# Low parts to VectorE, the residual sum earlier and fused, LayerNorm moments on ScalarE, in a two-block fp32 kernel

## The chip, the cores and the metric

One core of one Trainium2 chip. The metric is the device time of one execution in microseconds (us), the median of three runs. TensorE is PE in the profile, with PEld its weight loads; VectorE is DVE, ScalarE is ACT, GpSimd is POOL, and SyncE, which issues most DMAs, is SP.

## The reference, cut to what matters

Two residual blocks over x of shape (2048, 512), fp32: attention with a learned feature map, then an MLP over the token axis.

```python
h0 = layernorm(x)                                   # over 512 channels, eps 1e-5
q, k, v = split(h0 @ wqkv)                          # 32 heads of 16
phi(u) = concat(softmax(u @ w_phi), softmax(-u @ w_phi))
kv = phi(k)^T v ;  z = sum over tokens of phi(k)
o  = phi(q) kv / (phi(q) . z + 1e-6)
h  = x + o @ wo
u  = gelu(layernorm(h)^T @ w1 + b1)                 # (512, 1792), contraction over 2048 tokens
out = h + (u @ w2 + b2)^T
```

## The kernel before, in words

The 2048 tokens are 16 tiles of 128. Every fp32 product is made of three fp32r matmuls: an operand is split into a high part (a copy by ScalarE, rounded to fp32r) and a low part (operand minus high part), and `mm3` multiplies high by high, high by low and low by high. So every weight and activation costs one copy on ScalarE and one subtraction on VectorE or GpSimd.

The stages, in order: the weights of q, k and v are prepared; a loop over tiles makes the features of k and v and accumulates kv and z; a short stretch ends that loop; the attention loop makes h; then the token MLP runs to the end (w1 to 300 us and beyond, then w2, line 745).

**The end of the k loop.** z is kept as `zacc` (128 x 1024), summed over tiles. The last addition (line 481, VectorE) is followed by two TensorE products with ones (line 486) that sum over partitions, and ScalarE copies the result to `zB` (line 487). Ahead of it in GpSimd's queue stand the low parts of wo for two of its four slices (`wo_lo`, line 429), the other two stand a little later.

**The attention loop** runs `it` from 0 to 18. From the k loop's last call on and through this loop, the order on TensorE, VectorE, ScalarE and GpSimd is the order in which the code calls (a manual schedule); each engine works its queue in order and waits by semaphores. One iteration does a step for several tiles:

- `s_num(it-1)`, line 544: TensorE multiplies transposed features by kv into the PSUM tile `tn`; ScalarE copies the high part `oh` (548); VectorE makes the low part `ol` (553, called in `s_ol`).
- `s_wo(it-2)`: 12 matmuls (lines 61 to 63) of oh, ol with woh, wol into PSUM tile `po`, of which there is one.
- `s_tr(it)`, line 526: TensorE transposes features into `tn`, again one buffer, shared with s_num; so it waits for `ol`. ScalarE copies the result to `pht` (528).
- `lead`: `s_pq` (458, GpSimd multiplies the features by the weights `w`), `s_ez` (440, GpSimd multiplies features by zB), one `negate` (159, GpSimd), the next q projection on TensorE, one exponential on ScalarE (169).
- a list of VectorE steps, interleaved from two lists: `ol`; the reduction `tz` of ez (449) and five small steps that end in `w` (450 to 455); for a projected q tile the maximum `mx` (151), the minimum `mn` (152) and the shift `eq` = q - mx (144); two sums `smq` (214). The shift's other half is a ScalarE copy of the same PSUM tile (`eq`, line 146); it waits for the VectorE half, since both write one tile. Projections of q end when all 16 are made; the last one, of tile 15, is shifted in iteration 5.
- `s_hn(it-3)`: ScalarE normalizes h of tile it-3 into `hn` (583) and copies the high part `hs` (56); GpSimd makes the low part (57). It needs `s_rstd(it-3)`, two GpSimd operations on 128x1 (578, 579) called at the iteration's start.
- `s_h(it-2)`: VectorE adds po to x (line 568, `h`), SP stores it, VectorE takes the moments (571 to 575).
- `fill`: the first w1 products, 6 matmuls for one pair of column blocks and one token tile. Pair 0 starts in iteration 4; pair 1 starts in iteration 5, after the q projections, and takes over the two PSUM tiles `pu` of q tiles 14 and 15.
- `fill_load`: SP loads a piece of w1 (`wraw`), ScalarE makes `whi`, VectorE `wlo` (56, 57), two pieces at the end of iteration 2, one at the end of 4 and of 5, two of 6, and so on.

Of the kernel before, what the change touches and what calls it, by code (L numbers as in the profile page):

```python
# [9 lines left out]
F32 = mybir.dt.float32  # L10
F32R = mybir.dt.float32r
AF = mybir.ActivationFunctionType
ALU = mybir.AluOpType
# [4 lines left out]
P = 128  # L18
S, D, H, DH, F = 2048, 512, 32, 16, 1792
NT = S // P  # L20
KD = D // P
# [8 lines left out]
EPS = 1e-5  # L30
# [3 lines left out]
def block_kernel(ctx: ExitStack, tc: tile.TileContext, x, xT, wT, phic, wo, w1, b1, w2, b2,  # L34
                 kvmask, ident_in, out):
    nc = tc.nc

    cst = ctx.enter_context(tc.tile_pool(name="cst", bufs=1))
# [6 lines left out]
    b1s = cst.tile([P, NF], F32, name="b1s")  # L45
    b2s = cst.tile([P, NT], F32, name="b2s")
    r1 = cst.tile([P, NT], F32, name="r1")
    mv2 = cst.tile([P, NT, 2], F32, name="mv2")
    r2 = cst.tile([P, NT], F32, name="r2")
    cst.tile([P, 56], F32, name="pad")  # L50
    nc.vector.memset(ones, 1.0)
    nc.vector.memset(mhalf, -0.5)

    def split(hi, lo, src, lo_engine):

        nc.scalar.activation(hi, src, AF.Copy)  # L56
        return lo_engine.tensor_sub(lo, src, hi)  # L57

    def mm3(o, ah, al, bh, bl, first, last):

# [27 lines left out]
    zacc = wp.tile([P, NG, P], F32, name="zacc")  # L88
# [5 lines left out]
    X, XH, EQ, PK, VS, SQ, PS, W = {}, {}, {}, {}, {}, {}, {}, {}  # L94
# [41 lines left out]
    def logit_ops(src, e, pool):  # L136

        v = src.rearrange("p (j h d) -> p j h d", h=2, d=DH)
        ev = signs(e)
        mx = wk.tile([P, NPR, 2], F32, name="mx")  # L140
        mn = wk.tile([P, NPR, 2], F32, name="mn")

        def shift():
            nc.vector.tensor_sub(ev[:, :, 0], v, mx.unsqueeze(3).to_broadcast([P, NPR, 2, DH]))
            if pool:
                nc.scalar.activation(ev[:, :, 1], v, AF.Copy)  # L146
                MN.append((ev, mn))
            else:
                nc.vector.tensor_sub(ev[:, :, 1], mn.unsqueeze(3).to_broadcast([P, NPR, 2, DH]), v)

        return [lambda: nc.vector.tensor_reduce(mx, v, axis=AX.X, op=ALU.max),
                lambda: nc.vector.tensor_reduce(mn, v, axis=AX.X, op=ALU.min),
                shift]

    def negate():

        if MN:
            ev, mn = MN.pop(0)
            nc.gpsimd.tensor_sub(ev[:, :, 1], mn.unsqueeze(3).to_broadcast([P, NPR, 2, DH]), ev[:, :, 1])

    def run(*lists):

        for i in range(max(map(len, lists))):
            for ops in lists:
                if i < len(ops):
                    ops[i]()

    def exps(t, e):
        nc.scalar.activation(e, e, AF.Exp, scale=r1[:, t:t + 1])
# [1 line left out]
    def heads(e):  # L171
        return e.rearrange("p g (a d) -> p (g a) d", d=DH)
# [224 lines left out]
    for t in range(3, NT - 1):  # L397
        if t + 2 < NT:
            raw = load_x(t + 2)
# [22 lines left out]
    woh = w2p.tile([P, KD, D], F32R, name="woh")  # L422
    wol = w2p.tile([P, KD, D], F32R, name="wol")
# [2 lines left out]
        nc.scalar.activation(woh[:, j], WO[j], AF.Copy)  # L426

    def wo_lo(j):
        nc.gpsimd.tensor_sub(wol[:, j], WO[j], woh[:, j])

    WO = {}
    for j in range(KD):
# [24 lines left out]
    def s_pq(t):  # L457
        nc.gpsimd.tensor_mul(heads(EQ[t]), heads(EQ[t]), W[t].rearrange("p g c h -> p (g c h)").unsqueeze(2).to_broadcast([P, 2 * H, DH]))  # L458

    def lead(it, mm):  # L460

        if 0 <= it + 1 < NT:
            s_pq(it + 1)
        if 0 <= it + 3 < NT:
            s_ez(it + 3)
        negate()
        for _ in range(mm):
            q_mm()
        q_exp(0)
# [4 lines left out]
    k_norm(NT - 1, False)  # L474
    for j in range(KD):
        wo_hi(j)
    wo_lo(0)
    wo_lo(1)
    v_kv()
    run(q_logits(0))  # L480
    nc.vector.tensor_add(zacc, zacc, PK[NT - 1])
    negate()
    zB = big.tile([P, NG, P], F32, name="zB", tag="big")
    for g in range(2):
# [3 lines left out]
    q_exp(0)  # L488
    s_ez(0)
    s_ez(1)  # L490
    wo_lo(2)
    wo_lo(3)
    q_mm()
    v_kv()
    run(s_den(0))
# [34 lines left out]
    def s_kv():  # L530

        pt = ps_o.tile([P, 2, P], F32, name="po")
        for b in range(2):
            nc.tensor.transpose(pt[:, b, :], kvS[:, 2 * b:2 * b + 2, :].rearrange("p n f -> p (n f)"), ident)
        nc.scalar.activation(kvB, pt, AF.Copy)

    def s_num(t):

        pn = ps_t.tile([P, 2, 4, P], F32, name="tn")[:, :, 0:2]
        for b in range(2):  # L540
            for c in range(4):
                for r in range(2):
                    rows, cols = slice(64 * r, 64 * r + 64), slice(32 * c, 32 * c + 32)
                    nc.tensor.matmul(pn[cols, r, b, :], kvB[rows, b, cols], PHT[t][rows, 4 * b + c, :],  # L544
                                     start=True, stop=True, skip_group_check=True)
        oh = ak.tile([P, 2, 2, P], F32R, name="oh")
        ol = ak.tile([P, 2, 2, P], F32R, name="ol")
        nc.scalar.activation(oh, pn, AF.Copy)
        OS[t] = oh, ol, pn

    def s_ol(t):
        oh, ol, pn = OS[t]
        return [lambda: nc.vector.tensor_sub(ol, pn, oh)]
# [11 lines left out]
    def s_h(t):  # L565

        h = HT[t]
        nc.vector.tensor_add(h, PO.pop(t), h)  # L568
        nc.sync.dma_start(out[t * P:(t + 1) * P, :], h)
        st = ak.tile([P, 6], F32, name="st2")  # L570
        nc.vector.bn_stats(st, h)
        nc.vector.bn_aggr(mv2[:, t, :], st)
        VE[t] = ak.tile([P, 2], F32, name="ve2")
        nc.vector.tensor_scalar(VE[t][:, 0:1], mv2[:, t, 1:2], 1.0 + EPS, EPS * EPS, op0=ALU.mult, op1=ALU.add)
        nc.vector.tensor_scalar_mul(VE[t][:, 1:2], mv2[:, t, 0:1], -1.0)

    def s_rstd(t):
        nc.gpsimd.tensor_tensor(r2[:, t:t + 1], VE[t][:, 0:1], mhalf[:, :1], op=ALU.pow)
        nc.gpsimd.tensor_mul(VE[t][:, 1:2], VE[t][:, 1:2], r2[:, t:t + 1])
# [7 lines left out]
    w1v = w1.rearrange("(k p) f -> p k f", p=P)  # L587
    w2v = w2.rearrange("(k p) s -> p k s", p=P)

    def stream(src, k0, n, c0, w):  # L590

        raw = wf.tile([P, n, w], F32, name="wraw")
        wh_ = wf.tile([P, n, w], F32R, name="whi")
        wl_ = wf.tile([P, n, w], F32R, name="wlo")
        nc.sync.dma_start(raw, src[:, k0:k0 + n, c0:c0 + w])
        LO.append(split(wh_, wl_, raw, nc.vector).ins)
        return wh_, wl_

    PU, WI, LO = {}, {}, []
    FN, FL = [0] * (NF // 2), [0] * (NF // 2)  # L600

    def fill_load(p):
        if FL[p] < NT:
            WI[p, FL[p]] = stream(w1v, FL[p], 2, p * 256, 256)
            FL[p] += 2

    def fill(p, pool=None):

        t = FN[p]
        FN[p] = t + 1  # L610
        if FL[p] <= t:
            fill_load(p)
        if t == 0:
            PU[p] = [pool.tile([P, D], F32, name="pu", tag="pu") for _ in range(2)]
        a, b = WI[p, t - t % 2]
        for c in range(2):
            mm3(PU[p][c], a[:, t % 2, c * P:(c + 1) * P], b[:, t % 2, c * P:(c + 1) * P],
                HN[t][:, 0], HN[t][:, 1], t == 0, t == NT - 1)

    for it in range(NT + 3):  # L620
        if 0 <= it < NT:
            s_x(it)
        if 0 <= it - 3 < NT:
            s_rstd(it - 3)
        if 0 <= it - 1 < NT:
            s_num(it - 1)
        if 0 <= it - 2 < NT:
            s_wo(it - 2)
        if it == 1:
            run(q_logits(0))  # L630
            q_mm()
        if 0 <= it < NT:
            s_tr(it)
        if it == 0:
            s_kv()
        lead(it, 1)
        den = s_den(it + 2) if it + 2 < NT else []
        run((s_ol(it - 1) if 0 <= it - 1 < NT else []) + q_logits(1) + (q_sums(0) if it > 0 else []), den)
        if it > 0:
            negate()  # L640
        if 0 <= it - 3 < NT:
            s_hn(it - 3)
        if 0 <= it - 2 < NT:
            s_h(it - 2)
        if FN[0] <= it - LAG:
            fill(0, ps_f)
        for _ in range(2):
            if q["logits"] == NT and FN[1] <= it - LAG:
                fill(1, ps_q)
        for p in range(2):  # L650
            if it >= LAG - 2 and FL[p] <= FN[p] + 1:
                fill_load(p)
    ms.close()
    a2.close()
    aq.close()
# [100 lines left out]
    for n, (sp, p) in enumerate(STEPS):  # L756
        t = 2 * sp
# [15 lines left out]
        if not last:  # L773
# [6 lines left out]
            for i, add in enumerate((u3.unsqueeze(1).to_broadcast([P, 2, HD]), e)):  # L780
                nc.vector.scalar_tensor_tensor(ot[:, i], bank[2 + i], b2s[:, t + i:t + i + 1], add,  # L781
                                               op0=ALU.add, op1=ALU.add)
# [68 lines left out]
```

## Time and profile before

| | |
|---|---|
| three runs | 535.80, 535.86, 536.12 us; median 535.86 |
| the profiled execution | 535.76 us, of which 534.0 is the span from the first to the last instruction |
| granted TensorE clock, mean | 0.997 of full speed |
| busy: PE, DVE, ACT, POOL | 522.6, 393.5, 258.6, 236.6 us |
| HBM read, written | 46.81, 8.39 MB |

All times in rows are microseconds from the start of the span. A row of the timeline has start, duration, engine, line, operation, the tiles written and read, their shapes, how many instructions in succession it stands for, and in brackets the engine's idle time before it with what ended that. A row of the waits view has the waiting engine and line, what it waited for, the total, the number of waits and the longest.

### The profile page before, as it was taken

The page shows a single profiled execution, that of the slowest core. Times are in us where ns is not written, and L with a number is a line of the kernel's source. Part 1 is how long each engine was busy: PE and PEld are TensorE (multiplying, and loading weights), DVE is VectorE, ACT ScalarE, POOL GpSimd, SP SyncE. Part 2 cuts the span into 40 slices and gives each one's busy share as a digit, 9 for nine tenths or more (in the row PEclk, how much of TensorE's full clock was granted, in tenths as well). Part 3 has the DMA queues.
Part 4 walks back from the last instruction along what each step waited for, and adds up shares of the span by engine and source line. Part 5 has one row for each costly group of instructions (what it writes and reads, how often), then busy time and mean ns, then how long its engine had stood idle before and what let it go on. Part 6 is the DMA issues. An engine that isn't in the chain of part 4 may idle for free.

```text
span 534.0 us, 9892 instructions
## 1 busy us (share of the span) xinstructions
PE 522.6 (98%) x3872; PEld 450.4 (84%) x3872; DVE 393.5 (74%) x722; ACT 258.6 (48%) x406; POOL 236.6 (44%) x184
## 2 busy tenths in 40 slices
PE   8999999998999999999999999999999999999995
PEld 7888888886876777778788888888899999999995
DVE  6993999875699989986536523835768878888774
ACT  6998844434346555544546423525443343343340
POOL 2589699878978989985435000000001101100110
PEclk9999999999999999999999999999999999999998
DMA  8534300021302233333256333533014556536631
GB/s 315 196 113 118 99 21 21 1 78 63 97 4 86 73 101 118 100 121 118 91 166 179 98 100 97 160 107 91 20 41 108 139 149 144 133 119 140 138 80 40
DMA packets 45486, 55.84 MB, mean 105 GB/s; under 512 B 3968, under 2 KB 33024, under 8 KB 45440
## 3 DMA queue, kind: packets, MB, share of 16 engines
q1 hardware_dynamic: 43136, 51.38, 30.2%
q0 software_dynamic: 2016, 3.67, 5.1%
q8 instruction: 30, 0.49, 0.4%
q10 hardware_dynamic: 288, 0.17, 0.1%
q14 instruction: 16, 0.13, 0.1%
HBM read 46.81 MB, written 8.39 MB: 103 GB/s over the span
## 4 chain that ended last, share of the span: by engine, by line
PE 91%; DVE 5%; ACT 2%; issue 1%; POOL 0%; DVEq 0%; POOLq 0%
PE py L745 26%; PE pu L61 12%; PE pu L62 12%; PE pu L63 12%; PE po L61 3%; PE pv L62 3%; PE pv L63 3%; PE pv L61 3%; PE pk_ps L61 2%; PE pk_ps L63 2%; PE pk_ps L62 2%; PE tn L526 2%; PE po L62 2%; PE po L63 2%; PE kvp L205 2%; PE tn L544 1%
## 5 line engine op out<-in xcount | busy, mean ns | idle before, releaser
L57 DVE TENSOR_TENSOR wlo<-wraw,whi 128x512 fp32r<-128x512 f32 (+1 forms) x84 | 100.3, 1204 | 69.4 <-ACT whi L56 67.9
L56 ACT ACTIVATE whi<-wraw 128x512 fp32r<-128x512 f32 (+1 forms) x84 | 81.9, 987 | 127.1 <-PE py L745 73.8
L783 POOL DMA_DIRECT2D out<-ot x14 | 12.5, 1001 | 211.3 <-DVE ot L781 211.3
L745 PE MATMUL py<-uf,whi 128*128 128x256 f32 x560 | 96.2, 283 | 0.0
L61 PE MATMUL pu<-hs,whi 128*128 128x512 f32 x224 | 87.6, 394 | 0.6 <-ACT eq L146 0.6
L62 PE MATMUL pu<-hs,whi 128*128 128x512 f32 x224 | 87.2, 389 | 0.0
L63 PE MATMUL pu<-hs,wlo 128*128 128x512 f32 x224 | 86.8, 389 | 0.0
L745 PEld LDWEIGHTS py<-uf,whi 128*128 128x128 f32 x560 | 83.3, 192 | 0.0
L745 PE MATMUL py<-uf,wlo 128*128 128x256 f32 x280 | 69.9, 283 | 0.0
L61 PEld LDWEIGHTS pu<-hs,whi 128*128 128x128 f32 x224 | 42.1, 188 | 9.5 <-ACT eq L146 1.1
L745 PEld LDWEIGHTS py<-uf,wlo 128*128 128x128 f32 x280 | 49.7, 192 | 0.0
L63 PEld LDWEIGHTS pu<-hs,wlo 128*128 128x128 f32 x224 | 42.0, 188 | 8.8
L62 PEld LDWEIGHTS pu<-hs,whi 128*128 128x128 f32 x224 | 42.1, 188 | 8.2
L528 ACT ACTIVATE pht<-tn 128x512 f32<-128x512 f32 x32 | 17.4, 596 | 49.7 <-PE tn L526 49.7
L440 POOL TENSOR_TENSOR ez<-eq,zB 128x1024 f32<-128x1024 f32 x16 | 38.4, 2406 | 0.7 <-ACT zB L487 0.7
L745 PE MATMUL py<-un,whi 128*128 128x256 f32 x224 | 38.4, 283 | 0.0
L193 POOL TENSOR_TENSOR pk<-pk,sk 128x1024 f32<-128x1024 f32 x16 | 31.1, 1944 | 9.4 <-DVE sk L192 7.6
L745 PEld LDWEIGHTS py<-un,whi 128*128 128x128 f32 x224 | 33.2, 192 | 0.1
L458 POOL TENSOR_TENSOR eq<-eq,w 128x1024 f32<-128x1024 f32 x16 | 31.1, 1942 | 3.1 <-DVE w L455 3.1
L197 POOL TENSOR_TENSOR zacc<-zacc,pk 128x1024 f32<-128x1024 f32 x13 | 31.3, 2409 | 0.6
L57 POOL TENSOR_TENSOR hs<-hn,hs 128x512 fp32r<-128x512 f32 x16 | 20.6, 1291 | 21.1 <-ACT hs L56 21.1
L61 PE MATMUL po<-woh,oh 128*128 128x512 f32 x64 | 26.6, 416 | 1.0 <-DVE h L568 1.0
(161 smaller groups left out, 1144.3 us busy)
## 6 DMA issues: line engine op xcount, KB each, us to landing
wraw<-in_w SPq DMA_DIRECT2D x112, 256.0 KB, 2.8
xraw<-in_xT SPq DMA_DIRECT2D x16, 256.0 KB, 3.1
xh<-in_x SPq DMA_DIRECT2D x16, 256.0 KB, 2.7
h<-in_x SPq DMA_DIRECT2D x16, 256.0 KB, 2.9
out<-h SPq DMA_DIRECT2D x16, 256.0 KB, 2.2
out<-ot POOLq DMA_DIRECT2D x14, 256.0 KB, 4.8
wraw<-in_wT SPq DMA_DIRECT2D x12, 256.0 KB, 4.9
wo<-in_wo SPq DMA_DIRECT2D x4, 256.0 KB, 3.8
```

What stands on the lines that cost most here:

```text
L56: nc.scalar.activation(hi, src, AF.Copy)
L57: return lo_engine.tensor_sub(lo, src, hi)
L61: nc.tensor.matmul(o, ah, bh, start=first, stop=False)
L62: nc.tensor.matmul(o, ah, bl, start=False, stop=False)
L63: nc.tensor.matmul(o, al, bh, start=False, stop=last)
L193: nc.gpsimd.tensor_mul(heads(PK[t]), heads(PK[t]), sk.unsqueeze(2).to_broadcast([P, 2 * H, DH]))
L197: nc.gpsimd.tensor_add(zacc, zacc, PK[t])
L440: nc.gpsimd.tensor_mul(EZ[t], EQ[t], zB)
L458: nc.gpsimd.tensor_mul(heads(EQ[t]), heads(EQ[t]), W[t].rearrange("p g c h -> p (g c h)").unsqueeze(2).to_broadcast([P, 2 * H, DH]))
L528: nc.scalar.activation(PHT[t][:, half * 4:half * 4 + 4, :], ptr[:, half], AF.Copy)
L745: nc.tensor.matmul(o, a[x], b[:, y], start=start and i == 0, stop=stop and i == 2, skip_group_check=True)
L783: nc.gpsimd.dma_start(out[(t + i) * P:(t + i + 1) * P, :], flat(ot[:, i]), accum_op=ALU.add)
```

## The change

Five edits, all at the end of the k loop and in the attention loop.

1. The four low parts of wo are made by VectorE, not GpSimd, after the last addition to zacc; that addition is cut into two halves of 512 columns, one for each of the two products that follow.
2. h is made by one `scalar_tensor_tensor` that also writes the sum of its row (`accum_out`). It stands fourth in VectorE's list, behind ol and two more steps, where it stood behind the whole list.
3. `bn_stats`, `bn_aggr` and two small operations on VectorE go. ScalarE makes the moments in the next iteration (`s_moments`, called between s_num and s_wo, so between oh and pht in ScalarE's queue): one 128x1 copy, one pass of squares over 128x512 with its sum, one 128x1 operation. s_rstd is called behind s_pq.
4. The low parts of w1's pieces are not made when the piece is loaded but a step later (`flush`), directly behind h in VectorE's list, so in the iteration after the load.
5. Bookkeeping: a constant tile, a pad, `s_pq` called outside `lead`.

TensorE's order stays the same up to a few w1 products behind the loop, where the scheduler places them.

```diff
-    def wo_lo(j):
-        nc.gpsimd.tensor_sub(wol[:, j], WO[j], woh[:, j])
+    def wo_lo(j):
+        nc.vector.tensor_sub(wol[:, j], WO[j], woh[:, j])
...
-    wo_lo(0)
-    wo_lo(1)
     v_kv()
     run(q_logits(0))
-    nc.vector.tensor_add(zacc, zacc, PK[NT - 1])
+    for g in range(2):
+        nc.vector.tensor_add(zacc[:, 4 * g:4 * g + 4, :], zacc[:, 4 * g:4 * g + 4, :], PK[NT - 1][:, 4 * g:4 * g + 4, :])
+    for j in range(KD):
+        wo_lo(j)
     negate()
...
     s_ez(1)
-    wo_lo(2)
-    wo_lo(3)
...
     def s_h(t):
         h = HT[t]
-        nc.vector.tensor_add(h, PO.pop(t), h)
+        VE[t] = ak.tile([P, 4], F32, name="ve2", bufs=3)
+        nc.vector.scalar_tensor_tensor(h, PO.pop(t), 1.0, h, op0=ALU.mult, op1=ALU.add, accum_out=VE[t][:, 2:3])
         nc.sync.dma_start(out[t * P:(t + 1) * P, :], h)
-        st = ak.tile([P, 6], F32, name="st2")
-        nc.vector.bn_stats(st, h)
-        nc.vector.bn_aggr(mv2[:, t, :], st)
-        VE[t] = ak.tile([P, 2], F32, name="ve2")
-        nc.vector.tensor_scalar(VE[t][:, 0:1], mv2[:, t, 1:2], 1.0 + EPS, EPS * EPS, op0=ALU.mult, op1=ALU.add)
-        nc.vector.tensor_scalar_mul(VE[t][:, 1:2], mv2[:, t, 0:1], -1.0)
+
+    def s_moments(t):
+        junk = ak.tile([P, D], F32, name="hj", bufs=1)
+        nc.scalar.activation(VE[t][:, 1:2], VE[t][:, 2:3], AF.Copy, scale=-1.0 / D)
+        nc.scalar.activation(junk, HT[t], AF.Square, bias=VE[t][:, 1:2], accum_out=VE[t][:, 3:4])
+        nc.scalar.activation(VE[t][:, 0:1], VE[t][:, 3:4], AF.Identity, scale=(1.0 + EPS) / D, bias=eps2)
...
+    LATER = []
+    def flush():
+        while LATER:
+            wl_, raw, wh_ = LATER.pop(0)
+            LO.append(nc.vector.tensor_sub(wl_, raw, wh_).ins)
...
         nc.sync.dma_start(raw, src[:, k0:k0 + n, c0:c0 + w])
-        LO.append(split(wh_, wl_, raw, nc.vector).ins)
+        nc.scalar.activation(wh_, raw, AF.Copy)
+        LATER.append((wl_, raw, wh_))
...
-        if 0 <= it - 3 < NT:
-            s_rstd(it - 3)
         if 0 <= it - 1 < NT:
             s_num(it - 1)
+        if 0 <= it - 3 < NT:
+            s_moments(it - 3)
         if 0 <= it - 2 < NT:
             s_wo(it - 2)
...
+        if 0 <= it + 1 < NT:
+            s_pq(it + 1)
+        if 0 <= it - 3 < NT:
+            s_rstd(it - 3)
         lead(it, 1)
         den = s_den(it + 2) if it + 2 < NT else []
-        run((s_ol(it - 1) if 0 <= it - 1 < NT else []) + q_logits(1) + (q_sums(0) if it > 0 else []), den)
+        ops = turns((s_ol(it - 1) if 0 <= it - 1 < NT else []) + q_logits(1) + (q_sums(0) if it > 0 else []), den)
+        ops[3:3] = ([lambda: s_h(it - 2)] if 0 <= it - 2 < NT else []) + [flush]
+        run(ops)
         if it > 0:
             negate()
         if 0 <= it - 3 < NT:
             s_hn(it - 3)
-        if 0 <= it - 2 < NT:
-            s_h(it - 2)
```

More of the change, by code (lines that the diff above doesn't have):

```diff
@@ L47, in block_kernel @@
     r1 = cst.tile([P, NT], F32, name="r1")
-    mv2 = cst.tile([P, NT, 2], F32, name="mv2")
+    eps2 = cst.tile([P, 1], F32, name="eps2")
     r2 = cst.tile([P, NT], F32, name="r2")
-    cst.tile([P, 56], F32, name="pad")
+    cst.tile([P, 80], F32, name="pad")
     nc.vector.memset(ones, 1.0)
     nc.vector.memset(mhalf, -0.5)
+    nc.vector.memset(eps2, EPS * EPS)
     def split(hi, lo, src, lo_engine):
         nc.scalar.activation(hi, src, AF.Copy)
-        return lo_engine.tensor_sub(lo, src, hi)
+        lo_engine.tensor_sub(lo, src, hi)
     def mm3(o, ah, al, bh, bl, first, last):
@@ L159, in negate, with turns @@
             nc.gpsimd.tensor_sub(ev[:, :, 1], mn.unsqueeze(3).to_broadcast([P, NPR, 2, DH]), ev[:, :, 1])
+    def turns(*lists):
+        return [ops[i] for i in range(max(map(len, lists))) for ops in lists if i < len(ops)]
     def run(*lists):
[L163 to L166, printed above, removed]
+        for op in turns(*lists):
+            op()
     def exps(t, e):
@@ L460, in lead @@
     def lead(it, mm):
-        if 0 <= it + 1 < NT:
-            s_pq(it + 1)
         if 0 <= it + 3 < NT:
@@ L612, in fill @@
             fill_load(p)
+            flush()
         if t == 0:
@@ L652, in block_kernel @@
                 fill_load(p)
+    flush()
     ms.close()
```

## The prediction

> **What bounds the kernel now.** First the page's line of busy times, then the view of TensorE's waits cut to 115 to 290 us, the stretch that the change touches.
>
> ```profile
> PE 522.6 (98%) x3872; PEld 450.4 (84%) x3872; DVE 393.5 (74%) x722; ACT 258.6 (48%) x406; POOL 236.6 (44%) x184
> PE pk_ps L486 <- DVE zacc L481: 1.7, 1, 1.7
> PE po L61 <- DVE h L568: 1.0, 1, 1.0
> PE pu L61 <- ACT eq L146: 0.6, 1, 0.6
> PE tn L526 <- DVE ol L553: 0.5, 1, 0.5
> ```
>
> TensorE is busy for 522.6 of 534.0 us, and its order and work hardly change. So the gain can only come out of these four waits, 3.8 us together, and a loss only out of waits that the change makes. VectorE's 393.5 us matter only where a step of it is the last that TensorE waits for. I take the four in order of time. "Iteration" means `it`; a is the price, so far unknown, of writing the row sum beside h.
>
> **The end of the k loop.** The timeline there:
>
> ```profile
> 123.96 3.48 POOL L429 TENSOR_TENSOR wol<-wo,woh 128x512 fp32r<-128x512 f32 x2
> 124.03 2.28 DVE L481 TENSOR_TENSOR zacc<-zacc,pk 128x1024 f32<-128x1024 f32 x1
> 126.46 1.96 PE L486 MATMUL pk_ps<-zacc,ones 128*128 128x512 f32 x4 [1.69 <-DVE zacc L481]
> 131.57 1.22 DVE L449 TENSOR_REDUCE tz<-ez 128x64 f32<-128x1024 f32 x1 [5.25 <-POOL ez L440]
> 179.70 1.29 POOL L57 TENSOR_TENSOR hs<-hn,hs 128x512 fp32r<-128x512 f32 x1 [0.30 <-ACT hs L56]
> 180.18 1.36 DVE L57 TENSOR_TENSOR wlo<-wraw,whi 128x512 fp32r<-128x512 f32 x1
> ```
>
> The addition reads two SBUF tiles and takes 2.28 us. The last two rows show another such instruction: wlo starts while GpSimd's hs (179.70 to 180.99) runs and ends at 181.54, 0.55 us after that one's end. So a VectorE subtraction with two SBUF operands makes no headway while GpSimd works on SBUF. The addition at 124.03 overlaps GpSimd's wol in the same way. The change takes wol off GpSimd and cuts the addition in two. A half has 512 columns, for which a subtraction or addition takes 0.68 us (ol, below). TensorE waits for the first half alone: 124.03 + 0.68 + the 0.15 that lay between the addition's end (126.31) and the matmul (126.46) = 124.86, **1.6 us** earlier. The second half is there 0.6 later, before the second product. The four wol subtractions, four times 0.6, go into VectorE's idle time of 5.25 us ahead of tz at 131.57, and GpSimd loses the work. I cost them at nothing; without that cover they would put 2.4 us ahead of tz, which TensorE reaches only through w and the features, iterations later.
>
> From here I give times on the clock of before, without these 1.6 us, and add them in at the end.
>
> **The order within an iteration.** VectorE and ScalarE from 164 us on, iteration 3; the row of 409.09 is the form that h takes, without the sum; then groups of the same operations.
>
> ```profile
> 164.24 1.28 DVE L57 TENSOR_TENSOR wlo<-wraw,whi 128x512 fp32r<-128x512 f32 x2
> 165.44 0.68 DVE L553 TENSOR_TENSOR ol<-tn,oh 128x512 fp32r<-128x512 f32 x1
> 166.04 1.21 DVE L449 TENSOR_REDUCE tz<-ez 128x64 f32<-128x1024 f32 x1
> 167.16 0.68 DVE L151 TENSOR_REDUCE mx<-pu 128x32 f32<-128x512 f32 x1
> 167.76 0.18 DVE L450 SCALAR_TENSOR_TENSOR tz<-smq,tz 128x32 f32<-128x32 f32 x1
> 167.86 0.68 DVE L152 TENSOR_REDUCE mn<-pu 128x32 f32<-128x512 f32 x1
> 168.45 0.22 DVE L452 TENSOR_TENSOR tz<-smq,tz 128x64 f32<-128x64 f32 x1
> 168.59 0.68 DVE L144 TENSOR_TENSOR eq<-pu,mx 128x512 f32<-128x512 f32 x1
> 409.09 0.75 DVE L781 SCALAR_TENSOR_TENSOR ot<-py,b2s,e 128x512 f32<-128x512 f32 x1
> 163.54 0.61 ACT L548 ACTIVATE oh<-tn 128x512 fp32r<-128x512 f32 x1
> 167.43 1.09 ACT L528 ACTIVATE pht<-tn 128x512 f32<-128x512 f32 x2 [3.28 <-PE tn L526]
> 168.40 1.16 ACT L169 ACTIVATE eq<-eq,r 128x1024 f32<-128x1024 f32 x1
> 169.44 0.60 ACT L146 ACTIVATE eq<-pu 128x512 f32<-128x512 f32 x1
> 169.92 0.82 ACT L583 ACTIVATE hn<-h,ve,r 128x512 f32<-128x512 f32 x1
> 170.77 0.63 ACT L56 ACTIVATE hs<-hn 128x512 fp32r<-128x512 f32 x1
> 171.31 0.58 ACT L548 ACTIVATE oh<-tn 128x512 fp32r<-128x512 f32 x1
> L571 DVE BATCH_NORM_STATS2 st<-h 128x6 f32<-128x512 f32 x16 | 11.1, 695 | 0.5
> L113 ACT ACTIVATE sqj<-xh,st 128x512 f32<-128x512 f32 x16 | 11.5, 721 | 0.3
> L113 ACT ACTIVATION_READ_ACCUMULATOR sqj<-xh,st 128x1 f32 x16 | 3.0, 191 | 0.0
> ```
>
> Starts lie 0.6 apart for a 0.68 us instruction, so I add starts, not durations (h: 0.67).
>
> What goes: the moments on VectorE, 0.7 for bn_stats and some 0.4 for three small ones, about 1.1 us in each iteration, at the end of its list. It comes back on ScalarE as 0.72 for the squares, 0.19 for their sum and two operations on 128x1, at most 0.2 each by that last row: 1.3 us between oh and pht, where ScalarE idles 3.28 us now. As oh and pht come closer together below, some 1.9 us remain; cover to spare is 0.5 us, so I cost it at nothing. Without cover the exponential and the copy `eq` (146) would be that much later.
>
> What moves: h goes from behind the list to behind ol, tz and mx; wlo goes from before ol to behind h. So ol is earlier by wlo's time, and shift `eq` (144), and with it ScalarE's copy (146), later by h's 0.67 + a and wlo's 0.6 a piece. That copy is queued ahead of hn, hs, whi and the next oh, and oh is what the next ol and TensorE's next transpose wait for. SP's queue gets h's store earlier, which holds nothing up.
>
> For a, nothing in this profile shows a VectorE instruction that sums beside its output. The nearest rows: no surcharge (0.75 at 409.09), or ScalarE's 0.19 read; the far end is a second pass, 0.6. Nothing suggests less than none. I take 0.05 to 0.1. By itself: the Trainium skill ("VectorE: DVE Perf Modes", section "Two Vector instructions with no wait between them") states that such an operation is two instructions, the main one and a read of the accumulator; no row of before shows one on VectorE, and by it a would be nearer the 0.19.
>
> **Iterations 3 and 4.** GpSimd there, TensorE at two places, and a later pair of wlo:
>
> ```profile
> 162.70 1.06 POOL L159 TENSOR_TENSOR eq<-mn,eq 128x512 f32<-128x512 f32 x1 [1.07 <-ACT eq L146]
> 164.34 0.99 POOL L578 TENSOR_TENSOR r<-ve,mhalf 128x1 f32<-128x1 f32 x1 [0.58 <-DVE ve L575]
> 165.55 1.93 POOL L458 TENSOR_TENSOR eq<-eq,w 128x1024 f32<-128x1024 f32 x1
> 167.45 2.41 POOL L440 TENSOR_TENSOR ez<-eq,zB 128x1024 f32<-128x1024 f32 x1
> 170.12 1.06 POOL L159 TENSOR_TENSOR eq<-mn,eq 128x512 f32<-128x512 f32 x1 [0.26 <-PE pu L63]
> 172.87 0.55 POOL L578 TENSOR_TENSOR r<-ve,mhalf 128x1 f32<-128x1 f32 x1
> 174.57 1.04 PE L526 MATMUL tn<-ident,eq 128*128 128x128 f32 x8
> 186.82 0.50 PE L61 MATMUL pu<-hs,whi 128*128 128x512 f32 x1 [0.65 <-ACT eq L146]
> 197.66 1.98 DVE L57 TENSOR_TENSOR wlo<-wraw,whi 128x512 fp32r<-128x512 f32 x2 [0.84 <-ACT whi L56]
> ```
>
> VectorE in iteration 3: ol right behind oh at 164.2, tz 164.8, mx 165.9, h 166.5, first wlo 167.2 + a. TensorE's wait for h, 1.0 us, is thus gone by far. But GpSimd: its pq (458) no longer has rstd ahead of it, starts when the negate of 162.70 ends, at 163.76, and ends 165.7; rstd takes 0.77 where no wlo holds it (0.55 as at 172.87, and a second one of 0.2; 166.4), then ez 2.41, to 168.8. The first wlo comes 0.8 us into ez and, by the rows at 179.70 and 180.18, ends 0.55 behind it: 169.35; the second 169.9. The three small steps and mn between bring the shift to 170.7 to 171.4. Then ScalarE: copy 171.4, hn 171.9, hs 172.75, oh 173.3 to 173.9; VectorE's ol to 174.6; TensorE's transpose at 174.75, where it was 174.57 behind the stall. The wait for h has been replaced by one for ol, 0.2 more.
>
> **Iteration 5, the one that decides.** From ol at 173.9 the same sums, with no wlo in iteration 4, give (whi takes 0.55 more on ScalarE, since a piece was loaded): shift of tile 14 at 177.7 + a, copy 178.45 + a, hn, hs, whi, oh 180.85 + a to 181.45 + a, ol 181.5 + a, tz 182.1 + a, mx 183.2 + a, h 183.8 + a, wlo ready at **184.5 + 2a**. GpSimd: hs's low part 173.45 (1.29), pq 174.7, rstd 176.6, ez 177.35 to 179.75, negate to 180.8, hs 180.8, pq 182.0, rstd 183.9, ez(8) ready at **184.65**. Both need the same tiles' memory; whoever is first makes the other wait. They tie at a = 0.09.
>
> If wlo is first: done 185.1 + 2a, mn, small steps, shift to 186.6 + 2a, copy at 186.65 + 2a, the first w1 product that takes over that PSUM tile at 187.45 with a = 0.07, against 186.82: **+0.65**.
>
> **Later.** The wait at 200.38 for ol (0.5) came since two wlo, 1.98 us, stood ahead of it; now they stand behind: **-0.5**. Other iterations keep VectorE 1.1 us lighter and I find no new last wait; iteration 7 is within 0.1 us of one.
>
> The sum: -1.6 + 0.65 - 0.5 = -1.45, from 535.76 (1.76 around the span, unchanged) to **534.3 us**. The median of the runs stands 0.1 above that execution, so the sum is as good against it.
>
> **The rivals.**
>
> *ez first (slower side).* In iteration 5 ez(8) starts before wlo, so wlo waits to ez's end at 187.05 and ends at 187.6; the shift follows at 188.4, the copy at 189.1, the w1 product at 189.75, +2.9. The sum is -1.6 + 2.9 - 0.5 = +0.8: 536.5 us. It decides where 2a exceeds 0.18, or where GpSimd is 0.2 us ahead of my sums; with a of 0.19 or more it adds up to 0.7 (537.2). For it: the tie, and that iteration 3 shows wlo caught like this. Against: GpSimd, too, is held by VectorE's ol and wlo, and every such hold makes ez later. Beside it: the Trainium skill ("SBUF — State Buffer", section "SBUF: two separate sides") calls the pair of ports that VectorE and GpSimd share an exclusive lock that whoever starts first keeps for the whole instruction. The rows at 179.70 and 180.18 agree, and it speaks against putting wlo beside ez.
>
> *No hold at all.* If wlo in iteration 3 gets in ahead of ez(6) (GpSimd's negate ahead of pq held 0.8 us longer than I take), the shift is 1.4 us earlier there, the transpose at 174.57 waits for nothing and the w1 product comes 1.0 us earlier than forecast, less or no wait: -1.6 - 1.0 - 0.5 = -3.1, 532.7 us.
>
> *The halves bring nothing.* The change doesn't do what it says if the first product still waits for both halves, or if both stay as slow behind other GpSimd work. With both awaited the first part is -1.0, with none 0: 534.9 to 535.9 with wlo first, later with ez first.
>
> **How the numbers follow.** Wlo first 0.42, with its own range 533.6 to 535.0 (a from 0 to 0.1, cover of 0.5 used up or not); ez first 0.38, 536.0 to 537.2; no hold 0.12; the halves 0.05, the rest later still 0.03. The range holds the first three: 532.6 to 537.2. A measurement of this kernel tells some 0.2% from no change, 1.07 us about 535.86, so 534.8 to 536.9 is the same. Faster: 0.36 of the first, 0.12 of no hold, 0.48. Same: 0.06 of the first, 0.30 of ez first, 0.02 of the halves, 0.38. Slower: 0.08 of ez first and 0.06 of the rest, 0.14.
>
> **What would show it.** Right: the product behind zacc starts near 124.9; no wait of TensorE for h, one of 1 to 1.6 us at the transpose of 174 us (less 1.6 for the earlier start); wlo in iteration 3 ends 0.55 us after ez; in iteration 5 wlo starts before ez, and the wait for the copy 146 is the last before 290 us. The forecast is wrong if that wlo starts after ez (then a wait of about 3 us for 146), if h takes more than 0.95 us with its sum, or if pht waits for the squares.

## The result and the profile after

| | before | after |
|---|---|---|
| median of 12 executions | 535.99 us | 535.02 us |
| after / before | | 0.9981, 95% interval 0.9972 to 0.9990 |
| profiled execution, span | 535.76, 534.0 | 535.27, 533.5 |
| busy: PE, DVE, ACT, POOL | 522.6, 393.5, 258.6, 236.6 | 523.4, 382.5, 277.6, 228.3 |

The change gains 1.0 us, 0.5 to 1.5 by the interval. That is 0.19%, just inside the bound of 0.2% below which I had called a result "the same", though "no change" lies outside the interval. The forecast was 1.45 us.

TensorE's waits in the stretch from 115 to 290 us, as shown of before:

```profile
PE tn L525 <- POOL hs L58: 1.4, 1, 1.4
PE pu L62 <- ACT eq L147: 0.7, 1, 0.7
PE pk_ps L487 <- DVE zacc L480: 0.5, 1, 0.5
PE pu L64 <- DVE wlo L596: 0.2, 1, 0.2
```

The waits for h (1.0) and for ol near 200 us (0.5) are gone; that for zacc fell from 1.7 to 0.5. New are 1.4 us at a transpose and 0.2 at a w1 product. (The first line names hs, which ends at 174.16 by the profile. The transpose does not read hs; it takes over the tile that ol reads, and ol ended at 174.02, 0.14 ahead of it, the distance that lay between ol and the transpose of 200.38 before.) The rows behind them, in the timeline of after; lines have moved by one or two, h is L568, wlo L596, the shift L145:

```profile
125.05 1.29 DVE L480 TENSOR_TENSOR zacc<-zacc,pk 128x512 f32<-128x512 f32 x2 [0.41 <-POOL pk L195]
126.26 5.56 DVE L431 TENSOR_TENSOR wol<-wo,woh 128x512 fp32r<-128x512 f32 x4
125.89 1.10 PE L487 MATMUL pk_ps<-zacc,ones 128*128 128x512 f32 x2 [0.45 <-DVE zacc L480]
165.84 2.39 POOL L442 TENSOR_TENSOR ez<-eq,zB 128x1024 f32<-128x1024 f32 x1
166.57 0.08 DVE L568 DVE_READ_ACCUMULATOR h<-po,h 128x1 f32 x1
166.57 2.81 DVE L596 TENSOR_TENSOR wlo<-wraw,whi 128x512 fp32r<-128x512 f32 x2
170.14 0.68 DVE L145 TENSOR_TENSOR eq<-pu,mx 128x512 f32<-128x512 f32 x1
173.33 0.69 DVE L552 TENSOR_TENSOR ol<-tn,oh 128x512 fp32r<-128x512 f32 x1 [0.73 <-ACT oh L547]
174.16 0.30 PE L525 MATMUL tn<-ident,eq 128*128 128x128 f32 x1 [1.37 <-POOL hs L58]
183.75 0.69 DVE L596 TENSOR_TENSOR wlo<-wraw,whi 128x512 fp32r<-128x512 f32 x1
184.44 2.38 POOL L442 TENSOR_TENSOR ez<-eq,zB 128x1024 f32<-128x1024 f32 x1
186.55 0.50 PE L62 MATMUL pu<-hs,whi 128*128 128x512 f32 x1 [0.74 <-ACT eq L147]
192.31 2.39 POOL L442 TENSOR_TENSOR ez<-eq,zB 128x1024 f32<-128x1024 f32 x1
193.16 2.09 DVE L596 TENSOR_TENSOR wlo<-wraw,whi 128x512 fp32r<-128x512 f32 x1
195.31 0.50 PE L64 MATMUL pu<-hs,wlo 128*128 128x512 f32 x1 [0.17 <-DVE wlo L596]
```

In iteration 3 (166 us) ez is 0.7 us ahead of the pair of wlo, which takes 2.81 instead of 1.2; the shift, ScalarE's chain, ol and TensorE's transpose follow. In iteration 5 (184 us) wlo is 0.69 ahead of ez and takes 0.69. In iteration 6 (192 us) ez is ahead again, and a w1 product waits for that wlo.

Matmul by matmul, the start in after minus the start in before says where the time went. The profiled execution of after loses 0.64 us in its first 7 us, before any changed instruction (last section); without that the steps are: zacc -1.21, transpose of 166 us -0.21, wait for h -1.15, transpose of 174 us +1.53, copy +0.13, wlo at 195 us +0.45, ol at 200 us -0.66, some w1 products in another order near 280 us +0.07. Sum -1.05; the medians differ by 0.97. The step at zacc is -1.21 of it, all the other steps together +0.16. z_only and eps_pool below part the -1.21 into -1.57 for the first edit and +0.36 for the constant eps2, which belongs to the other edits; so those cost 0.5 us together.

### The profile page after: what moved, and what is told of

Read it like the earlier page. It is cut to its first block, busy times and chain, and to the rows that moved or that the text cites. A ratio compares the mean times of both kernels' runs of the same rounds, so it can differ in the third digit from the quotient of the medians.

```text
span 533.5 us, 9887 instructions
## 1 busy us (share of the span) xinstructions
PE 523.4 (98%) x3872; PEld 451.0 (85%) x3872; DVE 382.5 (72%) x680; ACT 277.6 (52%) x470; POOL 228.3 (43%) x180
## 4 chain that ended last, share of the span: by engine, by line
PE 90%; DVE 5%; ACT 3%; issue 1%; POOL 1%; DVEq 0%; ACTq 0%; POOLq 0%
PE py L761 26%; PE pu L62 12%; PE pu L64 12%; PE pu L63 11%; PE po L62 3%; PE pv L63 2%; PE tn L525 2%; PE pv L64 2%; PE pv L62 2%; PE pk_ps L62 2%; PE po L63 2%; PE po L64 2%; PE pk_ps L64 2%; PE pk_ps L63 2%; PE tn L543 2%; PE kvp L207 1%
## 5 line engine op out<-in xcount | busy, mean ns | idle before, releaser
L57 ACT ACTIVATE whi<-wraw 128x1792 fp32r<-128x1792 f32 x28 | 47.7, 1705 | 77.9 <-PE py L761 62.9
L596 DVE TENSOR_TENSOR wlo<-wraw,whi 128x512 fp32r<-128x512 f32 x56 | 46.3, 841 | 45.2 <-ACT whi L604 44.0
L58 DVE TENSOR_TENSOR wlo<-wraw,whi 128x1792 fp32r<-128x1792 f32 x28 | 56.6, 2023 | 17.8 <-ACT whi L57 17.8
L604 ACT ACTIVATE whi<-wraw 128x512 fp32r<-128x512 f32 x56 | 34.4, 627 | 45.6 <-PE pu L63 41.6
L442 POOL TENSOR_TENSOR ez<-eq,zB 128x1024 f32<-128x1024 f32 x16 | 39.5, 2474 | 0.1
```

The source lines that it names most:

```text
L442: nc.gpsimd.tensor_mul(EZ[t], EQ[t], zB)
L596: LO.append(nc.vector.tensor_sub(wl_, raw, wh_).ins)
L604: nc.scalar.activation(wh_, raw, AF.Copy)
```

## The experiments

Each ran against the kernel before in five rounds; the ratio is to before in the same rounds, with its 95% interval in brackets, and "after" is the median of 535.02.

**z_only: the first edit alone.** Before, with `wo_lo` on VectorE behind zacc, and zacc in two halves.

> The kernel before with the first edit alone: wo's low parts on VectorE behind the last addition to zacc, and that addition in two halves. If the first edit works by itself as the trace of after shows it, TensorE's wait for zacc (1.7 us) falls to between 0.1 and 0.5, and the three later waits (h 1.0, copy 0.6, ol 0.5) stay as before: 1.2 to 1.6 us faster than before, near 534.5. The rival: what TensorE gains there it gives back at the wait for h, since VectorE's and GpSimd's chains do not start earlier: near 535.9, with a wait for h of over 2 us.

Measured: 534.48 us, ratio 0.9970 (0.9958 to 0.9982), 0.5 below the median of the whole change. TensorE's waits in the same stretch, and its product behind zacc:

```profile
PE po L61 <- DVE h L567: 1.0, 1, 1.0
PE pu L61 <- ACT eq L146: 0.6, 1, 0.6
PE tn L525 <- DVE ol L552: 0.5, 1, 0.5
124.89 0.67 PE L487 MATMUL pk_ps<-zacc,ones 128*128 128x512 f32 x1
```

The product starts at 124.89, 1.57 earlier than before, and no later matmul loses any of it: the other three waits are what they were. The rival is out.

**z_whole: zacc in one piece, wol on VectorE.**

```diff
-    for g in range(2):
-        nc.vector.tensor_add(zacc[:, 4 * g:4 * g + 4, :], ...)
+    nc.vector.tensor_add(zacc, zacc, PK[NT - 1])
```

> The changed kernel with the addition to zacc in one piece, wo's low parts on VectorE still. Two causes share the first term: GpSimd no longer holds the addition (2.28 us against about 1.3), and TensorE waits for one half alone (0.6). If both count, this kernel loses 0.6 against after: 535.6, with the addition at about 1.25 us. If the halves bring nothing, 535.0; if the halves are all and GpSimd's hold was not the reason, the addition still takes over 2 us and the time is 536.2.

Measured: 535.36, ratio 0.9988 (0.9980 to 0.9997).

```profile
124.59 1.23 DVE L479 TENSOR_TENSOR zacc<-zacc,pk 128x1024 f32<-128x1024 f32 x1 [0.41 <-POOL pk L195]
```

The addition takes 1.23 us where it took 2.28 beside GpSimd's wol, so the hold that went is worth 1.05, of which a pause of VectorE (eps_pool, below) takes 0.37 back; TensorE's product gains 0.67 over before in this kernel and 1.21 in after, so the halves are 0.54. The whole kernel loses 0.34 against after, a little less than expected.

**z_undone: the change without its first edit.** `wo_lo` on GpSimd at its two old places, zacc whole.

> The changed kernel without the first edit (wo's low parts on GpSimd again, the addition whole). If the parts add up, it loses the 1.2 to 1.6 us of the first edit and stands at 536.1 to 536.6, that is at or a little above before: the other edits together are then worth -0.2 to +0.6. The rival: the attention loop's own edits bring the gain and this kernel stays near 535.0.

Measured: 537.80, ratio 1.0024 (1.0014 to 1.0035), more than expected. The view by windows has length, busy time of PE, PEld, DVE, ACT and POOL with the number of instructions, then the granted clock, DMA's busy share and its GB/s:

```profile
126.78 3.25 PE L486 MATMUL pk_ps<-zacc,ones 128*128 128x512 f32 x4 [2.03 <-DVE zacc L481]
127.00:129.00 2.00, 2.00 (x4) 0.73 (x4) 0.00 (x0) 0.60 (x1) 1.76 (x2) 0.57 0.00 0
129.00:132.00 3.00, 3.00 (x10) 2.09 (x9) 0.00 (x0) 1.64 (x2) 1.26 (x1) 0.72 0.00 0
```

The wait for zacc is back at 2.03 us, 0.34 more than in before (that same pause), and the granted clock then falls to 0.57 and 0.72 of full speed in these windows: the matmuls behind it lose another 1.65 us. It does not fall in every execution: of the 12, five took 536.17 to 536.77 at a mean clock of 0.997, as expected, and seven 537.77 to 539.02 at 0.994 or 0.995. The edits add up only where the clock holds.

**wlo_from_psum: the same two subtractions with one operand out of PSUM.**

```diff
+            other = PS[q['logits'] - 1].rearrange('p (k c) -> p k c', k=2) if len(LO) < 2 else wh_
-            LO.append(nc.vector.tensor_sub(wl_, raw, wh_).ins)
+            LO.append(nc.vector.tensor_sub(wl_, raw, other).ins)
```

> The changed kernel in which the two subtractions wlo of iteration 3 take their second operand from the PSUM tile pu instead of whi, so that only one operand lies in SBUF (these two low parts are wrong; the instructions, their size and order are the same). If VectorE is held by GpSimd's ez because of two SBUF operands, the pair takes 1.2 us instead of 2.81, the shift comes 1.6 earlier, and TensorE's wait at the transpose near 174 us (1.4) goes: 533.4 to 533.8. If any subtraction beside ez is that slow, or if the order alone (h and two wlo ahead of the shift) makes the wait, nothing changes: 535.0.

Measured: 533.16, ratio 0.9948 (0.9937 to 0.9960), 1.9 faster than after and a little faster than expected; between the traces the transpose is worth 1.50, and all else lies in the first 7 us (last section). The two rows overlap as in after:

```profile
165.26 2.40 POOL L442 TENSOR_TENSOR ez<-eq,zB 128x1024 f32<-128x1024 f32 x1
166.00 1.28 DVE L597 TENSOR_TENSOR wlo<-wraw,pu 128x512 fp32r<-128x512 f32 x2
168.03 0.68 DVE L145 TENSOR_TENSOR eq<-pu,mx 128x512 f32<-128x512 f32 x1
```

Same place, same ez, same sizes: 1.28 us with one SBUF operand, 2.81 with two. The wait of 1.4 us at the transpose is gone. It is the second SBUF operand that GpSimd's work holds up, not the order.

**ez_first: the prediction's slower rival, made to happen.** wlo of iteration 5 three steps later.

```diff
-        ops[3:3] = ([lambda: s_h(it - 2)] if 0 <= it - 2 < NT else []) + [flush]
-        run(ops)
+        ops[3:3] = [lambda: s_h(it - 2)] if 0 <= it - 2 < NT else []
+        at = 7 if it == 5 else min(4, len(ops))
+        run(ops[:at] + [flush] + ops[at:])
```

> The changed kernel with wlo of iteration 5 alone three steps later in VectorE's list (behind two small steps and mn, still ahead of the shift). In after it started at 183.75 us, 0.7 before GpSimd's ez at 184.44; here it is ready at about 184.6, so ez is first. If the prediction's slower rival has its price right, wlo is held to 187.4, the shift comes at 187.4 instead of 185.2, and the wait for the copy grows from 0.7 to about 2.9: 535.0 + 2.2 = 537.2, and up to 1.5 more if a wait that long lowers the granted clock. If nothing holds it, wlo is moved behind mn for nothing: 535.0.

Measured: 537.05, ratio 1.0025 (1.0014 to 1.0035).

```profile
183.77 2.39 POOL L442 TENSOR_TENSOR ez<-eq,zB 128x1024 f32<-128x1024 f32 x1
184.28 2.42 DVE L596 TENSOR_TENSOR wlo<-wraw,whi 128x512 fp32r<-128x512 f32 x1
PE pu L62 <- ACT eq L147: 2.5, 1, 2.5
```

wlo ends 0.54 behind ez, as the rows of before have it, and the wait for the copy is 2.5. In this trace all runs 0.3 us earlier than in after, so against it wlo is ready 0.8 later. A shift of one instruction by 0.8 us turns the change from 1.0 us faster into 1.2 us slower than before.

**h_last: h behind the list again.**

```diff
-        ops[3:3] = ([lambda: s_h(it - 2)] if 0 <= it - 2 < NT else []) + [flush]
-        run(ops)
+        ops[3:3] = [flush]
+        run(ops)
+        if 0 <= it - 2 < NT:
+            s_h(it - 2)
```

> The changed kernel with h behind VectorE's list again (wlo still late, moments on ScalarE). The list of iteration 3 then ends near 172.5 us, h at 173.1, and TensorE's products po, which start at 169.8 in after, wait 3.4 us for it; the wait of 1.4 at the next transpose goes, and so does part of the one for the copy (0.7). Sum +1.3 to +2.0: 536.3 to 537.0, and up to 1.5 more if so long a wait lowers the granted clock, as the kernel without the first edit showed after 2.0 us. The rival: since after only put one wait in the place of another, h's place is worth nothing: 535.0.

Measured: 548.24, ratio 1.0217 (1.0203 to 1.0231): far beyond the expectation.

```profile
PE po L62 <- DVE h L568: 10.1, 5, 3.4
173.00:178.00 5.00, 4.48 (x11) 3.51 (x12) 4.88 (x11) 1.82 (x6) 4.78 (x5) 0.50 0.28 107
```

The first wait is the 3.4 us that I expected, and the clock behind it is 0.50. What I left out: later lists hold a wlo that ez holds, too, and h behind it is late again, four times more, 6.7 us together. This trace is of the fastest of four executions (546.87); the other three, at 548.14 to 548.38, have a mean clock of 0.989 or 0.990 instead of 0.994.

**bn_back: the moments on VectorE again, behind its list.** `bn_stats`, `bn_aggr` and two small operations in place of `s_moments`; h a plain addition.

> The changed kernel with the moments on VectorE again, at the end of its list (bn_stats and three small steps; h without its sum, no pass of squares on ScalarE). VectorE idles 0.7 to 2.6 us ahead of ol in after, and the moments take 1.1: in iteration 4 ol comes up to 0.4 later, elsewhere nothing. So 535.0 to 535.4: the third edit is worth almost nothing by itself. Rivals: ScalarE's pass of 1.4 us is on the path, then this kernel is faster than 534.6; or VectorE's lighter list carries the gain, then it is slower than 535.8.

Measured: 538.68, ratio 1.0042 (1.0029 to 1.0056), 3.7 slower than after, and out of the expected range.

```profile
PE tn L526 <- DVE ol L553: 3.3, 4, 1.4
203.21 3.09 DVE L598 TENSOR_TENSOR wlo<-wraw,whi 128x512 fp32r<-128x512 f32 x2
208.20 0.68 DVE L575 BATCH_NORM_STATS2 st<-h 128x6 f32<-128x512 f32 x1
209.27 0.68 DVE L553 TENSOR_TENSOR ol<-tn,oh 128x512 fp32r<-128x512 f32 x1
```

I had checked iteration 4, where it costs little. In the iterations with a pair of wlo, the pair takes 3.1 us beside ez, the list ends late, and the 1.1 us of moments then put ol behind TensorE's need. In after there is just enough room. But matmul by matmul the waits make only some 1.6 of the 3.3 us by which this trace is longer than that of after; the other 1.7 come where no changed instruction runs. The same two matmuls of the k loop in after, then here:

```profile
18.39 0.39 PE L64 MATMUL pk_ps<-wkh,xs 128*128 128x512 f32 x1
115.19 0.39 PE L62 MATMUL pk_ps<-wkh,xs 128*128 128x512 f32 x1
```

```profile
18.24 0.39 PE L65 MATMUL pk_ps<-wkh,xs 128*128 128x512 f32 x1
116.58 0.39 PE L63 MATMUL pk_ps<-wkh,xs 128*128 128x512 f32 x1
```

They lie 96.80 us apart in after and 98.34 here: two 512-column products in succession start 0.231 us apart (the median) where they start 0.227 apart in every other trace, without a wait between them. Part of it comes back in the w2 part, where the matmuls from 390 to 526 us take 1.17 less than in after. The cause is open. What differs ahead of that loop is the tile mv2 (128 bytes of each partition), which this kernel has again without a smaller pad. So with the fourth edit in place the third holds off about 1.6 us of waits; what it is worth by itself was not run.

**wlo_now: the low parts made at the load again.** `stream` subtracts at once; the other edits stay.

> The changed kernel with the low parts wlo made when the piece is loaded, as before (the fourth edit undone; h third, moments on ScalarE). The two of iteration 2 then stand ahead of ol of tile 2, next to GpSimd's negate and pq (162.2 to 165.1 in after): if they are held there, the second ends near 166 us, ol near 166.4, and TensorE's transpose at 165.5 waits about 1; h comes near 168.6, still ahead of po at 169.8 to 170.8, and the wait of 1.4 at 174.2 is gone or small. The waits of after for the copy and for wlo go, the one near 200 us for ol (0.5) comes back. Sum 534.5, between 533.8 and 535.3. If the order alone counts and nothing is held, 533.5; if this order is the one that h third needs, as the theory behind the fourth edit would have it, over 536.

Measured: 541.96, ratio 1.0111 (1.0096 to 1.0127). I had the first iterations right (the pair ends at 166.26, ol at 166.87) and all the later ones wrong:

```profile
PE tn L525 <- POOL ve L580: 7.3, 5, 2.3
197.76 3.71 DVE L605 TENSOR_TENSOR wlo<-wraw,whi 128x512 fp32r<-128x512 f32 x2 [2.16 <-ACT whi L604]
198.55 2.38 POOL L460 TENSOR_TENSOR eq<-eq,w 128x1024 f32<-128x1024 f32 x1
201.40 0.68 DVE L552 TENSOR_TENSOR ol<-tn,oh 128x512 fp32r<-128x512 f32 x1
```

The pair meets pq, and ol behind it comes so late that five transposes wait. (The first line names ve, GpSimd's second rstd operation; as with hs above, it is ol that TensorE waits for, which ends at 202.08, 0.15 ahead of the transpose.) In before the pair stood at the same place (197.66) and took 1.98 us. The difference on GpSimd is that rstd, two operations on 128x1, came there ahead of pq, and the third edit put pq first.

**wlo_now_rstd: the same with rstd ahead of pq.**

```diff
+        if 0 <= it - 3 < NT:
+            s_rstd(it - 3)
         if 0 <= it + 1 < NT:
             s_pq(it + 1)
-        if 0 <= it - 3 < NT:
-            s_rstd(it - 3)
```

> The kernel with the low parts made at once (wlo_now), in which GpSimd computes rstd ahead of pq again, as before; rstd now waits for ScalarE's moments, so pq starts about a microsecond later. If wlo_now lost its 7 us since the pair of wlo met pq (2.4 us of GpSimd's work) where before it met the two small steps of rstd, the pair near 198 us takes 1.8 to 2 us instead of 3.7, ol comes 1.7 earlier, the waits of 1.4 to 2.3 at five transposes go but for some 0.5, and the time is 534.8 to 536. If the waits come from the pair's place ahead of ol alone, or if the later pq costs as much, it stays at 540 to 542.

Measured: 533.84, ratio 0.9961 (0.9947 to 0.9974), 8 us faster for two small operations called earlier, 1.2 faster than after, and faster than the 534.8 to 536 that I expected.

```profile
195.22 1.98 DVE L605 TENSOR_TENSOR wlo<-wraw,whi 128x512 fp32r<-128x512 f32 x2 [2.15 <-ACT whi L604]
197.53 0.55 POOL L579 TENSOR_TENSOR r<-ve,mhalf 128x1 f32<-128x1 f32 x1 [1.49 <-ACT ve L576]
```

GpSimd now idles 1.49 us for ScalarE's moments, and the pair goes through in that gap. So with rstd ahead of pq the change does without its fourth edit; the place of rstd made that edit necessary.

**eps_pool: the constant eps2 written by GpSimd, not VectorE.** `nc.gpsimd.memset(eps2, ...)`.

> The changed kernel with the new constant eps2 written by GpSimd, so that VectorE has the same number of instructions ahead of the k loop as before. In after, VectorE's reduction sk at 115.6 us starts 0.46 us behind ScalarE's end, in before and with the first edit alone 0.10, and the addition to zacc is that much later. If one instruction more in VectorE's queue moves a pause of the queue to that place, the 0.36 us come back: 534.65, TensorE's wait for zacc 0.1. If the pause belongs to something else, 535.0.

Measured: 534.28, ratio 0.9962 (0.9950 to 0.9975). VectorE's reduction sk in after and here; ScalarE's operation that it waits for ends at 115.13 and 114.38:

```profile
115.59 1.22 DVE L193 TENSOR_REDUCE sk<-pk 128x64 f32<-128x1024 f32 x1 [2.42 <-ACT pk L171]
```

```profile
114.48 1.22 DVE L193 TENSOR_REDUCE sk<-pk 128x64 f32<-128x1024 f32 x1 [2.06 <-ACT pk L171]
```

0.46 us against 0.10. Behind the first 7 us this is the only step between the two traces, and 0.36 of the 0.74 between the medians. With one instruction less ahead of it the pause is gone, and with it the wait for zacc. It is 0.46 or 0.47 in all ten traces that write eps2 on VectorE, and 0.10 in the four that do not (before, z_only, eps_pool, best2). What VectorE's queue does in the pause was not found, nor whether it is the number of instructions ahead that counts.

**best1 and best2: versions made from these readings.** The diff is the loop of best2; best1 has 4 in place of `len(ops)`. best1 puts wlo behind the shift in iterations 3 and 5, ahead of ol in 6, behind h from 7 on; best2 adds eps2 on GpSimd, and wlo at the end of the list from 7 on.

```diff
+        if it == 6:
+            flush()
-        ops[3:3] = ([lambda: s_h(it - 2)] if 0 <= it - 2 < NT else []) + [flush]
-        run(ops)
+        ops[3:3] = [lambda: s_h(it - 2)] if 0 <= it - 2 < NT else []
+        at = 8 if it < 6 else len(ops)
+        run(ops[:at] + [flush] + ops[at:])
```

> A version made from the readings: as after, but the low parts wlo stand behind the shift in iterations 3 and 5, ahead of ol in iteration 6, and behind h from 7 on, so that no shift and no w1 product waits for a wlo that GpSimd holds. TensorE's waits of 1.4 (transpose), 0.7 (copy), and 0.2 (wlo) should go: 535.0 - 2.3 = 532.7, or 532.2 to 533.2. The rival: a wlo held at its new place delays w or ol as much, and the time stays near 534.5 to 535.

> best1 with two further edits: eps2 written by GpSimd (the pause of VectorE ahead of the addition to zacc goes, 0.36), and the low parts from iteration 7 on at the end of VectorE's list, where GpSimd's ez has ended (the wait of 0.4 for ol near 205 us goes). 533.15 - 0.75 = 532.4. The rival: at the end of the list the low parts meet hs's low part on GpSimd and hold the next ol: 533 or more, with waits for ol at several transposes.

Measured: best1 533.15, ratio 0.9944 (0.9931 to 0.9956); best2 532.37, ratio 0.9936 (0.9923 to 0.9948), 3.4 us faster than before and 2.6 faster than after. In best2 one wait of TensorE is left between 115 and 290 us:

```profile
PE pu L62 <- ACT eq L147: 0.6, 1, 0.6
```

This wait did not go in best1 either, though I had expected it to, and a wait of 0.4 for ol came there, which best2 removes. For the first: the copy in best1 starts at 184.35 where the shift ended at 183.67, since ScalarE's exponential, queued ahead of it, ends at 184.46.

## Why the prediction was right, and where it was off

The sign, the range and the likeliest case held: the first edit carries the gain (alone it is 0.5 us better than the whole change), the wait for h is replaced by one for ol, and in iteration 5 wlo came ahead of ez. Step by step, on the clock of before (0.64 us taken off after's times for its slow start, 1.21 added for zacc):

- *zacc, -1.6.* The mechanism was exact: with this edit alone the product starts at 124.89 where I had 124.86. In the whole change it was -1.21. The step that failed is "124.03" as the addition's start: the constant eps2, which I costed nowhere, put a pause of 0.36 us in VectorE's queue ahead of the reduction that zacc hangs on.
- *Iteration 3.* I had the transpose at 174.75; it came at 174.73. The pair of wlo ended 1.15 behind ez, as worked out (169.9 against 168.8); wlo_from_psum shows the cause. What I said of iteration 5, that wlo and ez need "the same tiles' memory", is wrong: wlo reads wraw and whi, ez reads eq and zB, and the hold came all the same. The Trainium skill ("SBUF — State Buffer", section "SBUF: two separate sides") calls the shared ports an exclusive lock, taken by a GpSimd operation, or by a VectorE operation with two SBUF inputs where GpSimd's reads SBUF; this case agrees, with 2.81 us for two SBUF operands and 1.28 for one.
- *Iteration 5, +0.65.* Measured +0.30: -0.21 and -1.15 for two waits that went, +1.53 for the transpose and +0.13 at the copy. One term that was mis-sized is a, the price of the row sum: h takes 0.685 us on the mean, the read of its sum 0.083, and the next instruction starts with the read (166.57), so a is 0 where I had 0.07, counted twice. The other 0.2 is in the chain ahead of it: ol came at 181.38 where I had 181.5, wlo 0.60 behind h instead of 0.67. The Trainium skill's rule that such an operation is two instructions ("VectorE: DVE Perf Modes", section "Two Vector instructions with no wait between them") shows in the rows, at no cost here. I called the race a tie, 184.5 + 2a against 184.65. In the rows wlo is 0.69 ahead of ez, but half of that is wlo's own hold on the operation ahead of ez:

```profile
183.93 0.56 POOL L580 TENSOR_TENSOR ve<-ve,r 128x1 f32<-128x1 f32 x1
```

  It takes 0.19 in the iterations around it. Without the hold ez starts at 184.07, or 184.64 on the clock of before, as worked out (ez_first, 0.3 us earlier throughout, has it at 183.77). So wlo won by 0.32.
- *The slower rival*, ez first: forecast 536.5 with 537.2 as its far end; made to happen it gave 537.05. ez_first is not that rival to the letter: mn and two small steps, 0.75 us, stand ahead of its wlo, and behind that of the rival. On the clock of before its w1 product comes 2.04 later than in before; the rival had 2.9, or 2.15 without those steps. So the price of the hold was right; that 537.05 lies so near to the far end is in part luck, since zacc gained 0.4 less than forecast. The chance of 0.38 looks too high afterwards, since an a of 0 breaks the tie.
- *Later iterations, -0.5 and "no new last wait".* The wait at 200 us went (-0.66). The second half failed: in iteration 6 wlo meets ez as in iteration 3, and a w1 product waits, +0.45. I had followed wlo's hold only where it delays the shift, not to the w1 product that reads wlo.
- *ScalarE's moments at nothing.* Between oh and pht in iteration 4, the tightest place (the squares, and pht):

```profile
173.42 0.72 ACT L575 ACTIVATE hj<-h,ve 128x512 f32<-128x512 f32 x1
175.27 1.09 ACT L527 ACTIVATE pht<-tn 128x512 f32<-128x512 f32 x2 [0.70 <-PE tn L525]
```

  All four operations take from 173.19 to 174.56, 1.4 us, and 0.70 us of idle time are left: right. But that VectorE's relief is worth nothing was right only for the path as a whole: bn_back shows it holding off about 1.6 us of waits.

Terms: +0.39 at zacc, -0.35 up to the copy, +0.45 at wlo, -0.16 at ol, +0.07 late: 0.4 us between the forecast of -1.45 and -1.05. Two errors of the same size, in opposite directions, lie inside the 0.4; that the sum came this near is in part luck.

## What to carry to other kernels

An operation moved from GpSimd to VectorE, or moved in time, has to be laid against the other engine's list: with two SBUF operands, the one that starts second makes no headway until the first ends (a 128x512 subtraction then ends about 0.55 us behind it). Here a move of 0.8 us decided between 535.0 and 537.1, one of two 128x1 operations between 533.8 and 542.0. When a change is made of several edits, measure each alone: here one edit of five made the gain, and the others cost 0.5 us together, though taking one of them back by itself cost up to 13 (h_last). Follow a delayed result to every reader, not only to the next step of the chain that you watch.

## What the runs showed of the hardware

- After a wait of TensorE of 2.03 us (z_undone) the granted clock was 0.50 from 127.3 to 130.7 us, after 3.41 (h_last) 0.50 from 172.8 to 179.6. After 2.48 (ez_first) and 2.26 (wlo_now) it stayed at full in the profiled executions. But as with z_undone, ez_first differs from one execution to the next: eight of 11 took 536.59 to 537.18 at a mean clock of 0.997, three 537.97 to 539.18 at 0.995 or 0.996. So a wait of two to two and a half microseconds may or may not cost the clock, in the same kernel, and h_last lost more to the clock near 174 us (2.2 us over 12 matmuls) than many an edit moves.
- The first microseconds are not the same in all executions. From 5.4 to 6.6 us, before any changed instruction, the windows of before and of after:

```profile
5.40:6.60 1.20, 1.20 (x11) 1.20 (x12) 1.12 (x4) 0.71 (x2) 0.00 (x0) 1.00 1.04 400
```

```profile
5.40:6.60 1.20, 1.20 (x6) 1.20 (x7) 0.69 (x2) 0.27 (x2) 0.00 (x0) 1.00 0.94 346
```

  TensorE works on 11 matmuls in the first and 6 in the second. The clock column shows 1.00 in both, but the trace's entries of the granted clock only begin at 5.17 us in before and at 6.77 in after, and there the rate steps up: the 128-column matmuls start 0.21 us apart ahead of it and 0.11 behind it. So the clock was very likely at half ahead of these entries. They begin between 3.93 and 6.91 us in the 14 traces; what decides it is not shown. The 0.64 us are kept to the end. The 12 executions of after fall into two groups, 534.57 to 534.86 and 535.18 to 535.51, with the median of 535.02 in the gap and the profiled execution in the second; that this start is what parts them is likely, not shown.
- One instruction in VectorE's queue, some 115 us ahead, came with a pause of 0.36 us on the path: in all ten traces that have it, in none of the four that do not.
- The same matmuls started 0.231 us apart in one kernel (bn_back) and 0.227 in all others, 1.5 us over the k loop, at a full granted clock; the cause is open.
